# Second stage, first pass: the float32 weights of the products down are asked for after the next pair's first products up

## The chip, the cores and the metric

One core of one Trainium2 chip runs the whole program. The metric is the device time of one execution in microseconds (us), the median of several runs.

## The reference

Linear attention with an exponential feature map, then a two-layer network with a leaky activation, then a mixture of four experts whose outputs are weighted per token. The change lies in the last part:

```python
def _moe2_ref(x, domain_probs, w1, w2):
    N, D = x.shape              # 2304, 512
    E = w1.shape[0]             # 4 experts of 1024 hidden units
    p = domain_probs / (domain_probs.sum(-1, keepdims=True) + 1e-09)
    out = np.zeros((N, D), dtype=np.float32)
    for e in range(E):
        h = np.maximum(x @ w1[e], 0.0)
        out += p[:, e:e + 1] * (h @ w2[e])
    return out
```

## The kernel before

The program has two stages: attention and the first network, then the four experts. The second stage goes over the 2304 tokens in three passes (i = 0, 1, 2) of 768 tokens, each as two halves r of 384. The 4096 hidden units of all experts are 32 chunks of 128. Two chunks form one f (0 to 15), two f form a pair gp (0 to 7), so a pair has a group of four chunks.

`up2(i, f)` (L923) computes the hidden values of two chunks for both token halves with seven products in place of eight, in the order 1, 5, 6, 2, 7, 3, 4. Each is six matmuls of TensorE (L934) into a bank of PSUM. Products 1, 6, 7 and 4 add up in one bank (pb), 5 and 3 in another (pd). In between ScalarE copies partial sums out: p1 (L952) before product 6 may write that bank again, p5 (L955), and u1 (L958) before product 7. VectorE adds them (`total`, L947) to c11, c22 and c12; c22 reads pb before product 4 writes there. `down2(i, gp, r, ...)` (L969) multiplies the hidden values of a pair by its four chunks of weights down (L981) and adds the result, scaled per token, to the output (L990, L992).

All operands are split into a rounded high part and a low rest, so every weight exists twice. In the first pass the weights come as float32: `weights_down(0, c)` (L859) loads a chunk into a raw tile (L867; written `w<-wdn` in the rows), ScalarE casts it to the high part, VectorE subtracts to get the low part (`split`, L237 and L240), and both are stored to DRAM for the later passes (L1020). `weights_up(0, f)` (L824) does the like for an f with two loads into raw tiles (L835), seven casts on ScalarE (L843) and eleven operations on GpSimd (L844 to L854). The raw tiles of both come from one pool of five (L759). The finished weights down of a group go into one of two sets of four places (`down_place`, L811): chunks 8k to 8k+4 into tiles named whd and wld, 8k+5 to 8k+7 into a part of Xh, so the casts into `Xh<-w` are of such chunks. Later passes load the finished weights (L830, L864).

The order of instructions on each engine is set when the program is built, by a scheduler that goes by the order in which the source asks for the work, and takes what is ready in its own reckoning. SP issues all loads and stores in one order. The main loop (L1015 to L1034) asks, for each f: up2, the weights up of f + 2, the stores that are due, then a down2 of one half; after the odd f it asks for the four chunks of the next pair.

Of the kernel before, what the change touches and what calls it, by code (L numbers as in the profile page):

```python
# [41 lines left out]
NPAIR = E * NF2 // 2  # L42
# [161 lines left out]
def fused(ctx: ExitStack, tc: tile.TileContext, qT, kT, v_main, v_tail, w_phi, alpha, probs, w64, wup, wdn, out):  # L204
# [30 lines left out]
    def split(src, hi, lo, hi_eng, lo_eng):  # L235
        if hi_eng is nc.scalar:
            nc.scalar.copy(hi, src)  # L237
        else:
            hi_eng.tensor_copy(hi, src)
        lo_eng.tensor_tensor(lo, src, f32(hi), ALU.subtract)  # L240
# [97 lines left out]
    with ExitStack() as st1:  # L338
# [232 lines left out]
        for p in range(len(pairs)):  # L571
# [44 lines left out]
            for h in range(3):  # L616
                pr_ = RANK["Q"] + p + 0.1 * h
                pm, n = (("pmt", (p,)), 1) if h == 2 else (("pmq", (p, h)), NM)
# [161 lines left out]
    def inputs(i, part):  # L780

        a = lambda r, c: acc_of(slice(2 * c, 2 * c + 2), (2 * i + r) * BLK2, BLK2)
        tt = nc.vector.tensor_tensor
        if part == 0:
            x_op(1, a(0, 0))
            x_op(4, a(1, 1))
            tt(a(1, 1), a(1, 0), a(1, 1), ALU.add)
            x_op(5, a(1, 1))
            tt(a(1, 0), a(1, 0), a(0, 0), ALU.subtract)
            tt(a(0, 0), a(1, 1), a(0, 0), ALU.subtract)  # L790
            x_op(6, a(0, 0))
            x_op(2, a(0, 1))
            tt(a(0, 1), a(0, 1), a(0, 0), ALU.subtract)
        else:
            x_op(7, a(1, 0))
            x_op(3, a(0, 1))
# [14 lines left out]
    def down_place():  # L811

        at = turn[1] % 8
        turn[1] += 1
        if at < 5:
            p_ = wa[1] if at < 4 else wb[1]
            return [p_.tile([P, DM], F32R, name="w" + n + "d") for n in "hl"]
        o = 16 * BLK2 + (at - 5) * 2 * DM
        return [XF[:, o + r * DM:o + (r + 1) * DM] for r in range(2)]

    def raw_tile():
        return rpool.tile([P, DM], F32, name="w")

    def weights_up(i, f):  # L824

        w = {k: up_place().rearrange("p (r c) -> p r c", r=2) for k in SEQ}
        uw[i, f] = w
        if i:
            for j, k in enumerate(SEQ):
                nc.sync.dma_start(f32(w[k]).rearrange("p r c -> p (r c)"), wsu[f][:, j])  # L830
            return
        b = {}
        for r in range(2):
            t = raw_tile()
            nc.sync.dma_start(t, wup[f, :, r])  # L835
            for n, h in zip(((11, 21), (22, 12))[r], range(2)):
                b[n] = t[:, h * 2 * P:(h + 1) * 2 * P]
        sums = [wtpool.tile([P, DM], F32, name=f"ts{r}") for r in range(2)]
        lo = lambda k: sums[k // 6][:, k % 2 * 2 * P:(k % 2 + 1) * 2 * P]
        tt = nc.gpsimd.tensor_tensor  # L840

        def parts(k, src):
            nc.scalar.copy(w[k][:, 0], src)  # L843
            tt(w[k][:, 1], src, f32(w[k])[:, 0], ALU.subtract)  # L844
            stores.append((f, wsu[f][:, SEQ.index(k)], f32(w[k]).rearrange("p r c -> p (r c)")))

        parts(1, b[11])
        tt(lo(5), b[12], b[11], ALU.subtract)
        tt(lo(6), b[22], lo(5), ALU.subtract)
        parts(5, lo(5))  # L850
        tt(lo(4), b[21], lo(6), ALU.subtract)
        parts(6, lo(6))
        parts(2, b[21])
        tt(lo(7), b[12], b[22], ALU.subtract)  # L854
        parts(7, lo(7))
        parts(3, b[22])
        parts(4, lo(4))

    def weights_down(i, c):  # L859
        w = down_place()  # L860
        dw[i, c] = w
        if i:
            for r in range(2):
                nc.sync.dma_start(f32(w[r]), wsd[c][:, r])  # L864
            return
        t = raw_tile()
        nc.sync.dma_start(t, wdn[c])  # L867
        split(t, *w, nc.scalar, nc.vector)
        for r in range(2):
            stores.append((c // 4 * 2 + 1, wsd[c][:, r], f32(w[r])))  # L870
# [13 lines left out]
    for s, (grp, blk) in enumerate(steps):  # L884
# [5 lines left out]
        for i in range(1, GRP):  # L890
# [7 lines left out]
            if todo and (blk or s == 0) and not (grp == 0 and len(todo) <= 2):  # L898
                n, half = todo.pop(0)
# [23 lines left out]
    def up2(i, f):  # L923
        ps = {k: None for k in ("pa", "pb", "pd")}
        t = lambda name: tpool.tile([P, BLK2], F32, name=name)
        w = uw.pop((i, f))

        def product(k, name, start, stop):
            if start:
                ps[name] = ps_u.tile([P, BLK], F32, name="up")[:, :BLK2]  # L930
            n = 0
            for kt in range(2):
                for r, x in ((0, 0), (0, 2), (1, 0)):
                    nc.tensor.matmul(ps[name], w[k][:, r, kt * P:(kt + 1) * P], slots[k][:, x + kt],  # L934
                                     start=start and n == 0, stop=stop and n == 5, skip_group_check=True)
                    n += 1

        def g(c, r, src):
            o = free.pop(0)
            gh, gl = (o[:, j * BLK2:(j + 1) * BLK2] for j in range(2))  # L940
            nc.scalar.activation(gh, src, AF.Relu)  # L941
            nc.vector.scalar_tensor_tensor(gl, src, 0.0, f32(gh), ALU.max, ALU.subtract)  # L942
            gs[2 * f + c, r] = gh, gl, o

        def total(name, x, out):
            o = t(out)
            nc.vector.tensor_tensor(o, ps[name], x, ALU.add)  # L947
            return o

        product(1, "pb", True, False)  # L950
        p1 = t("p1")
        nc.scalar.copy(p1, ps["pb"])  # L952
        product(5, "pd", True, False)
        p5 = t("p5")
        nc.scalar.copy(p5, ps["pd"])  # L955
        product(6, "pb", False, False)
        u1 = t("u1")
        nc.scalar.copy(u1, ps["pb"])  # L958
        product(2, "pa", True, True)
        g(0, 0, total("pa", p1, "c11"))  # L960
        product(7, "pb", False, False)
        c22 = total("pb", p5, "c22")
        product(3, "pd", False, True)
        g(1, 0, total("pd", u1, "c12"))
        product(4, "pb", False, True)
        g(0, 1, ps["pb"])
        g(1, 1, c22)

    def down2(i, gp, r, by_tile):  # L969

        chunks = range(4 * gp, 4 * gp + 4)
        ps = {}

        def product(c, m):
            if c == chunks[0]:
                ps[m] = ps_d.tile([P, BLK], F32, name="dn")
            gh, gl, _ = gs[c, r]
            wh, wl = dw[i, c]
            sl = slice(m * P, (m + 1) * P)
            for k, (w, x) in enumerate(((wh, gh), (wl, gh), (wh, gl))):  # L980
                nc.tensor.matmul(ps[m], x[:, sl], w, start=c == chunks[0] and k == 0, stop=c == chunks[-1] and k == 2)  # L981

        def add2(m):
            tok = (2 * i + r) * TB + m
            if (gp, r, m) == (0, 0, 0):
                acc2[i] = apool.tile([P, 2 * TB, DM], F32, name="acc2")
            av = acc2[i][:, r * TB + m]
            pe = pr[:, tok, 2 * gp // EP:2 * gp // EP + 1]
            if gp == 0:
                nc.vector.tensor_scalar_mul(av, ps[m], pe)  # L990
            else:
                nc.vector.scalar_tensor_tensor(av, ps[m], pe, av, ALU.mult, ALU.add)  # L992
            if gp == NPAIR // 2 - 1:
                nc.sync.dma_start(out[tok * P:(tok + 1) * P], av)

        if by_tile:
            for m in range(TB):
                for c in chunks:
                    product(c, m)
                add2(m)  # L1000
        else:
            for c in chunks:
                for m in range(TB):
                    product(c, m)
            for m in range(TB):
                add2(m)
        for c in chunks:
            free.append(gs.pop((c, r))[2])

    ups = [(i, f) for i in range(NPASS) for f in range(NPAIR)]  # L1010
# [3 lines left out]
    for n, (i, f) in enumerate(ups):  # L1014
        gp = f // 2  # L1015
        up2(i, f)
        if n + 2 < len(ups):
            weights_up(*ups[n + 2])
        while stores and stores[0][0] <= n + 1:
            nc.sync.dma_start(*stores.pop(0)[1:])  # L1020
        if f % 2 == 0:
            if gp:
                down2(i, gp - 1, 1, False)
        else:
            down2(i, gp, 0, False)
            if n + 1 < len(ups):
                i2, f2 = ups[n + 1]
                for c in range(4):
                    weights_down(i2, 2 * f2 + c)
            if gp == NPAIR // 2 - 1:  # L1030
                down2(i, gp, 1, True)
                if i + 1 < NPASS:
                    inputs(i + 1, 0)
                    inputs(i + 1, 1)  # L1034
# [39 lines left out]
```

## Time and profile before

| | us |
|---|---|
| median of 3 runs (1321.79 to 1323.01) | 1322.16 |
| the profiled execution | 1321.2 |
| its span, first to last instruction | 1319.1 |
| TensorE busy with matmuls | 1307.2 (99%) |
| VectorE, ScalarE, GpSimd busy | 758.1, 454.6, 274.2 |
| matmuls of the products up and down, second stage, in the chain that ended last | 25% and 29% of the span |

The second stage's first pass runs from about 566 to 819 us of the span. A matmul's shown duration overlaps the next one's, so the pace is read from the distance between starts. In the rows PE is TensorE, DVE VectorE, ACT ScalarE, POOL GpSimd, and SPq an entry of SP's DMA queue.

### The profile page before, as it was taken

How to read it: one execution, taken by the hardware profiler on the slowest of the kernel's cores; microseconds unless marked ns; L12 is line 12 of the kernel's file. 1: busy time of each engine (PE TensorE's matmuls, PEld its weight loads, DVE VectorE, ACT ScalarE, POOL GpSimd, SP SyncE). 2: the span in 40 equal slices, each digit the busy share in tenths (PEclk: the TensorE clock that was granted, in tenths of full speed). 3: DMA queues.
4: the chain of work that ended last, by engine and by line, in shares of the span. 5: the costliest groups of instructions: out<-in, count | busy, mean ns of one | idle time of the engine just before them, and what ended most of it. 6: DMA issues, size and time to landing. Idle time of an engine off the chain costs nothing.

```text
span 1319.1 us, 21240 instructions
## 1 busy us (share of the span) xinstructions
PE 1307.2 (99%) x8184; PEld 1118.5 (85%) x8184; DVE 758.1 (57%) x1283; ACT 454.6 (34%) x979; POOL 274.2 (21%) x292
## 2 busy tenths in 40 slices
PE   9999999999999999998999999999999999999998
PEld 5577776888888888897999998999999899999997
DVE  7996866999697456664455446433343453333433
ACT  6775655332131121253444433222222232222221
POOL 5562412120020130274566620000000000000000
PEclk9999999999999999999999999999999999999999
DMA  5431220322020030098677666666666565566641
GB/s 168 123 110 49 55 56 12 112 81 96 17 72 9 9 119 1 25 320 287 246 254 257 251 221 197 227 188 194 195 188 192 176 224 175 176 186 190 192 135 48
DMA packets 102469, 192.36 MB, mean 146 GB/s; under 512 B 13920, under 2 KB 14048, under 8 KB 102368
## 3 DMA queue, kind: packets, MB, share of 16 engines
q1 hardware_dynamic: 102368, 191.00, 44.5%
q8 instruction: 65, 1.06, 0.3%
q14 instruction: 36, 0.29, 0.1%
HBM read 140.10 MB, written 50.86 MB: 145 GB/s over the span
## 4 chain that ended last, share of the span: by engine, by line
PE 93%; DVE 3%; DMA 1%; ACT 1%; issue 1%; SPq 0%; POOL 0%; DVEq 0%; ACTq 0%; POOLq 0%
PE dn L981 29%; PE up L934 25%; PE up L292 12%; PE dn L313 12%; PE mm L313 3%; PE mm L292 2%; PE kv L447 2%; PE bank L522 2%; PE bank L403 2%; DVE m L419 1%; PE bank L532 1%; PE bank L503 1%; DMA w<-wdn 1%; PE kv L456 0%; DVE pmk L425 0%
## 5 line engine op out<-in xcount | busy, mean ns | idle before, releaser
L981 PE MATMUL dn<-whd,Xh 128*128 128x512 f32 x720 | 231.4, 390 | 0.0
L992 DVE SCALAR_TENSOR_TENSOR acc<-dn,pr,acc 128x512 f32<-128x512 f32 x126 | 88.7, 749 | 190.9 <-PE dn L981 190.9
L934 PE MATMUL up<-Xl,wlu 128*128 128x384 f32 x864 | 158.8, 335 | 2.7 <-DVE c L947 2.6
L981 PEld LDWEIGHTS dn<-whd,Xh 128*128 128x128 f32 x720 | 135.1, 188 | 27.1
L934 PEld LDWEIGHTS up<-Xl,wlu 128*128 128x128 f32 x864 | 150.2, 188 | 4.3 <-DVE c L947 3.8
L947 DVE TENSOR_TENSOR c<-up,p 128x384 f32<-128x384 f32 x96 | 53.5, 557 | 174.1 <-PE up L934 171.5
L981 PE MATMUL dn<-Xh 128*128 128x512 f32 x648 | 151.8, 389 | 0.0
L981 PEld LDWEIGHTS dn<-Xh 128*128 128x128 f32 x648 | 121.6, 188 | 25.5
L981 PE MATMUL dn<-wld,Xh 128*128 128x512 f32 x360 | 140.8, 391 | 0.0
L952 ACT COPY p<-up 128x384 f32<-128x384 f32 x48 | 23.1, 481 | 325.7 <-PE up L934 325.6
L934 PE MATMUL up<-Xl,whu 128*128 128x384 f32 x576 | 111.7, 334 | 1.1 <-ACT p L952 1.1
L941 ACT ACTIVATE Xh<-c 128x384 fp32r<-128x384 f32 x144 | 75.6, 526 | 80.0 <-DVE c L947 80.0
L934 PEld LDWEIGHTS up<-Xl,whu 128*128 128x128 f32 x576 | 101.2, 188 | 1.4 <-ACT p L952 1.4
L292 PE MATMUL up<-Xl,whu 128*128 128x512 f32 (+1 forms) x272 | 99.1, 364 | 0.0
L292 PE MATMUL up<-Xh,whu 128*128 128x512 f32 (+1 forms) x272 | 99.1, 364 | 0.0
L313 PE MATMUL dn<-gh,wld 128*128 128x512 f32 (+1 forms) x272 | 99.1, 364 | 0.0
L313 PE MATMUL dn<-gh,whd 128*128 128x512 f32 (+1 forms) x272 | 99.1, 364 | 0.0
L313 PE MATMUL dn<-gl,whd 128*128 128x512 f32 (+1 forms) x272 | 99.0, 364 | 0.0
L292 PE MATMUL up<-Xh,wlu 128*128 128x512 f32 (+1 forms) x272 | 99.0, 364 | 0.0
L942 DVE SCALAR_TENSOR_TENSOR Xh<-c,Xh 128x384 fp32r<-128x384 f32 x144 | 86.0, 599 | 5.4
L237 ACT CAST gh<-t 128x512 fp32r<-128x512 f32 (+1 forms) x68 | 38.6, 569 | 145.1 <-DVE t L304 143.0
L981 PEld LDWEIGHTS dn<-wld,Xh 128*128 128x128 f32 x360 | 67.5, 188 | 13.0
(171 smaller groups left out, 2222.4 us busy)
## 6 DMA issues: line engine op xcount, KB each, us to landing
whu<-wsu SPq DMA_DIRECT2D x96, 256.0 KB, 3.4
wlu<-wsu SPq DMA_DIRECT2D x96, 256.0 KB, 3.1
st<-w SPq DMA_DIRECT2D x24, 512.0 KB, 3.2
wsu<-whu SPq DMA_DIRECT2D x48, 256.0 KB, 3.1
wsu<-wlu SPq DMA_DIRECT2D x48, 256.0 KB, 2.3
Xh<-wsd SPq DMA_DIRECT2D x48, 256.0 KB, 3.8
wld<-wsd SPq DMA_DIRECT2D x40, 256.0 KB, 3.0
whd<-wsd SPq DMA_DIRECT2D x40, 256.0 KB, 3.3
```

The lines of the kernel that those rows point to most:

```text
L237: nc.scalar.copy(hi, src)
L292: nc.tensor.matmul(ps[:, :bn], a[:, cs], x[:, cc, t0:t0 + bn], start=n == 0, stop=n == 3 * CC - 1)
L313: nc.tensor.matmul(ps, w[:, sl], g, start=start and k == 0, stop=stop and k == 2)
L403: nc.tensor.matmul(ps[h][:, i], x[r, i * P:(i + 1) * P], w0[r, h], start=True, stop=True, tile_position=(h * D, 0), skip_group_check=True)
L447: nc.tensor.matmul(kv[h * D + o:h * D + o + 32, 0], a[:, o:o + 32], e, start=i == 0, stop=i == NM, tile_position=(0, h * D + o), skip_grou ...
L522: nc.tensor.matmul(nd[o:o + 32, :HS], tl["kvt", p][:, a:a + 32], tl["qe", p][:, h, s, c * HS:(c + 1) * HS], start=s == 0, stop=s == 1, til ...
L934: nc.tensor.matmul(ps[name], w[k][:, r, kt * P:(kt + 1) * P], slots[k][:, x + kt], start=start and n == 0, stop=stop and n == 5, skip_grou ...
L941: nc.scalar.activation(gh, src, AF.Relu)
L942: nc.vector.scalar_tensor_tensor(gl, src, 0.0, f32(gh), ALU.max, ALU.subtract)
L947: nc.vector.tensor_tensor(o, ps[name], x, ALU.add)
L981: nc.tensor.matmul(ps[m], x[:, sl], w, start=c == chunks[0] and k == 0, stop=c == chunks[-1] and k == 2)
L992: nc.vector.scalar_tensor_tensor(av, ps[m], pe, av, ALU.mult, ALU.add)
```

## The change

In the first pass, the four chunks of pair gp are asked for after up2 of its even f, after the weights up of f + 2 and the stores, ahead of the second down2 of pair gp - 1. Before, they were asked for after the first down2 of pair gp - 1, so ahead of that up2. The first pass's pair 0 and the later passes are asked for as before.

```diff
         if f % 2 == 0:
+            if gp and i == 0:
+                for c in range(4):
+                    weights_down(i, 4 * gp + c)
             if gp:
                 down2(i, gp - 1, 1, False)
         else:
             down2(i, gp, 0, False)
-            if n + 1 < len(ups):
+            if n + 1 < len(ups) and (i or gp == NPAIR // 2 - 1):
                 i2, f2 = ups[n + 1]
                 for c in range(4):
                     weights_down(i2, 2 * f2 + c)
```

On TensorE the order stays as it was. Three places show what moves, all for chunks 12 to 15, whose conversion falls around up2 of f = 5.

SP's queue, before, from the load of chunk 12 to that of chunk 15. `w<-wdn` is the load of a chunk, `wsu6<-` and `wsd12<-` are stores of finished weights; in brackets stand the counters that the entry waits for (DMAHW: an earlier transfer; Pool, Activation, DVE: work of GpSimd, ScalarE, VectorE).

```order
L867 DMA w_7190<-wdn 128x512 [waits DMAHW2_49]
L1020 DMA wsu6_63<-whu_6955 128x512 [waits DMAHW3_49,Pool_49]
L1020 DMA wsu6_63<-whu_6956 128x512 [waits DMAHW4_49,Pool_49]
L1020 DMA wsu6_63<-wlu_6957 128x512 [waits DMAHW5_49,Pool_49]
L1020 DMA wsu6_63<-wlu_6958 128x512 [waits DMAHW6_49,Pool_49]
L867 DMA w_7194<-wdn 128x512 [waits DMAHW7_49]
L1020 DMA wsu6_63<-wx_6959 128x512 [waits DMAHW0_49,Pool_49]
L1020 DMA wsu6_63<-wx_6960 128x512 [waits DMAHW1_49,Pool_49]
L867 DMA w_7198<-wdn 128x512 [waits DMAHW2_49]
L1020 DMA wsu6_63<-whu_6961 128x512 [waits DMAHW3_49,Pool_49]
L1020 DMA wsd12_85<-whd_7188 128x512 [waits DMAHW4_49,Activation_49]
L867 DMA w_7202<-wdn 128x512 [waits DMAHW5_49,DVE_49]
```

The same place after, from the second store of wx to behind the load of chunk 14.

```order
L1020 DMA wsu6_63<-wx_6936 128x512 [waits DMAHW1_49,Pool_49]
L867 DMA w_7293<-wdn 128x512 [waits DMAHW2_49]
L1020 DMA wsu6_63<-whu_6937 128x512 [waits DMAHW3_49,Pool_49]
L1020 DMA wsd12_85<-whd_7291 128x512 [waits DMAHW4_49,Activation_49]
L867 DMA w_7297<-wdn 128x512 [waits DMAHW5_49,DMAHW2_49,DVE_49]
L1020 DMA wsd12_85<-wld_7292 128x512 [waits DMAHW6_49]
L1020 DMA wsd13_86<-Xh_122 128x512 [waits DMAHW7_49,Activation_49]
L867 DMA w_7301<-wdn 128x512 [waits DMAHW5_49,DMAHW0_49,DVE_49]
L1020 DMA wsu7_64<-whu_7100 128x512 [waits DMAHW1_49,Pool_49]
```

The first load moved behind the stores of wx, and the second and third now wait for VectorE: each goes into the raw tile that the chunk before it has left. The fourth load (not shown) stands behind six stores of f = 7.

ScalarE, before, at the start of up2 of f = 5: casts of chunks 12 to 15, then that up2's copies.

```order
L237 CAST whd_7188<-w_7190 128x512
L237 CAST Xh_122<-w_7194 128x512
L237 CAST Xh_122<-w_7198 128x512
L237 CAST Xh_122<-w_7202 128x512
L952 COPY p1_7050<-up_7043 128x384
L843 CAST whu_7108<-w_7115 128x256
L955 COPY p5_7059<-up_7052 128x384
L843 CAST whu_7109<-ts0_7119 128x256
L958 COPY u1_7067<-up_7043 128x384
```

The same place after.

```order
L237 CAST whd_7291<-w_7293 128x512
L237 CAST Xh_122<-w_7297 128x512
L952 COPY p1_7042<-up_7035 128x384
L843 CAST whu_7100<-w_7107 128x256
L955 COPY p5_7051<-up_7044 128x384
L843 CAST whu_7101<-ts0_7111 128x256
L958 COPY u1_7059<-up_7035 128x384
L843 CAST whu_7102<-ts1_7112 128x256
L237 CAST Xh_122<-w_7301 128x512
```

The cast of chunk 14 moved behind the copies, that of chunk 15 further back; chunks 12 and 13 are still ahead of p1.

VectorE, before, there: subtractions of chunks 12 to 15, three evictions of a down2 (L992), and the sums of up2.

```order
L240 TENSOR_TENSOR wld_7189<-w_7190,whd_7188 128x512
L240 TENSOR_TENSOR Xh_122<-w_7194,Xh_122 128x512
L240 TENSOR_TENSOR Xh_122<-w_7198,Xh_122 128x512
L992 SCALAR_TENSOR_TENSOR acc2_6546<-dn_7001,pr_119,acc2_6546 128x512
L992 SCALAR_TENSOR_TENSOR acc2_6546<-dn_7005,pr_119,acc2_6546 128x512
L992 SCALAR_TENSOR_TENSOR acc2_6546<-dn_7009,pr_119,acc2_6546 128x512
L240 TENSOR_TENSOR Xh_122<-w_7202,Xh_122 128x512
L947 TENSOR_TENSOR c11_7076<-up_7069,p1_7050 128x384
L947 TENSOR_TENSOR c22_7086<-up_7043,p5_7059 128x384
```

The same place after.

```order
L240 TENSOR_TENSOR wld_7292<-w_7293,whd_7291 128x512
L992 SCALAR_TENSOR_TENSOR acc2_6546<-dn_6993,pr_119,acc2_6546 128x512
L992 SCALAR_TENSOR_TENSOR acc2_6546<-dn_6997,pr_119,acc2_6546 128x512
L992 SCALAR_TENSOR_TENSOR acc2_6546<-dn_7001,pr_119,acc2_6546 128x512
L240 TENSOR_TENSOR Xh_122<-w_7297,Xh_122 128x512
L947 TENSOR_TENSOR c11_7068<-up_7061,p1_7042 128x384
L240 TENSOR_TENSOR Xh_122<-w_7301,Xh_122 128x512
L947 TENSOR_TENSOR c22_7078<-up_7035,p5_7051 128x384
```

The subtraction of chunk 13 moved behind the evictions, that of chunk 14 between c11 and c22. Chunks 16 to 19, 20 to 23 and 24 to 27 read the same at f = 7, 9 and 11; chunks 28 to 31 keep the old order. For chunks 4 to 7 (up2 of f = 2) three casts stand ahead of p1 and the fourth ahead of p5; for chunks 8 to 11 (f = 3) one cast stands ahead of p1.

## Rows read from the trace of the kernel before

**Rows 1.** The page, part 1: busy us, share of the span, instructions.
```profile
PE 1307.2 (99%) x8184; PEld 1118.5 (85%) x8184; DVE 758.1 (57%) x1283; ACT 454.6 (34%) x979; POOL 274.2 (21%) x292
```
**Rows 2.** Windows: length; busy PE, PEld, DVE, ACT, POOL (count); clock; DMA share; GB/s.
```profile
604.40:616.00 11.60, 7.90 (x43) 7.22 (x43) 5.81 (x11) 6.60 (x16) 4.12 (x5) 1.00 0.65 230
616.00:800.00 184.00, 184.00 (x925) 166.66 (x925) 87.01 (x138) 76.13 (x176) 92.92 (x112) 1.00 0.71 249
```
**Rows 3.** Timeline of PE, f = 3: start, duration, operation, [idle before, releaser].
```profile
604.44 1.23 PE L934 MATMUL up<-x,whu 128*128 128x384 f32 x6
...
607.82 1.31 PE L934 MATMUL up<-Xl,whu 128*128 128x384 f32 x6 [1.10 <-ACT p L952]
...
614.85 1.31 PE L934 MATMUL up<-Xl,wlu 128*128 128x384 f32 x6 [2.60 <-DVE c L947]
```
**Rows 4.** Timeline of ACT, f = 3.
```profile
605.58 1.81 ACT L237 CAST whd<-w 128x512 fp32r<-128x512 f32 x3 [8.35 <-DMA w<-wdn]
607.29 0.47 ACT L952 COPY p<-up 128x384 f32<-128x384 f32 x1
...
612.99 0.62 ACT L237 CAST whd<-w 128x512 fp32r<-128x512 f32 x1 [2.98 <-DMA w<-wdn]
```
**Rows 5.** Timeline of DVE, f = 3.
```profile
613.64 0.69 DVE L240 TENSOR_TENSOR wld<-w,whd 128x512 fp32r<-128x512 f32 x1 [2.80 <-ACT whd L237]
```
**Rows 6.** The chain of waits around f = 3: start, duration, what.
```profile
600.58 4.92 DMA w<-wdn
...
607.83 5.13 DMA w<-wdn
```
**Rows 7.** Timeline of PE, f = 2: products 1; 6 and 2; 7 and 3.
```profile
588.94 1.23 PE L934 MATMUL up<-x,whu 128*128 128x384 f32 x6
...
591.04 2.24 PE L934 MATMUL up<-Xl,wlu 128*128 128x384 f32 x12
593.12 2.24 PE L934 MATMUL up<-Xl,wx 128*128 128x384 f32 x12
```
**Rows 8.** Timeline of ACT, f = 2.
```profile
591.67 0.41 ACT L843 CAST whu<-ts 128x256 fp32r<-128x256 f32 x1
592.34 0.48 ACT L958 COPY u<-up 128x384 f32<-128x384 f32 x1 [0.26 <-PE up L934]
```
**Rows 9.** Timeline of PE, f = 5, product 1.
```profile
639.71 1.23 PE L934 MATMUL up<-x,whu 128*128 128x384 f32 x6
```
**Rows 10.** Timeline of SP's queue ahead of f = 5.
```profile
631.34 2.35 SPq L1020 DMA_DIRECT2D wsu<-wx  x2
633.74 0.42 SPq L867 DMA_DIRECT2D w<-wdn  x1
```
**Rows 11.** Timeline of ACT, f = 5.
```profile
641.03 0.48 ACT L952 COPY p<-up 128x384 f32<-128x384 f32 x1 [0.49 <-PE up L934]
```
**Rows 12.** Timeline of DVE, f = 5: three evictions, and c22.
```profile
639.14 2.06 DVE L992 SCALAR_TENSOR_TENSOR acc<-dn,pr,acc 128x512 f32<-128x512 f32 x3
...
645.19 0.56 DVE L947 TENSOR_TENSOR c<-up,p 128x384 f32<-128x384 f32 x1 [0.47 <-PE up L934]
```
**Rows 13.** Line 867, one load, issued at 664.8: issue ns; us to landing.
```profile
L867 SPq DMA_DIRECT2D w<-wdn x1: 426/426/426, 664.8 to 664.8; - x1
...
DMA to landing us min/median/max: 3.2/3.2/3.2
```
**Rows 14.** Line 867, four loads in a row, chunks 4 to 7.
```profile
L867 SPq DMA_DIRECT2D w<-wdn x4: 328/426/451, 576.2 to 581.9; - x4
...
DMA to landing us min/median/max: 2.7/3.0/3.4
```
**Rows 15.** Timeline of POOL: an L854, and the end of f = 3's part.
```profile
573.06 0.74 POOL L854 TENSOR_TENSOR ts<-w 128x256 f32<-128x256 f32 x1 [0.66 <-DMA w<-wup]
...
583.82 1.18 POOL L844 TENSOR_TENSOR wlu<-ts,wlu 128x256 fp32r<-128x256 f32 x1
```
**Rows 16.** Timeline of SP's queue: the last store of f = 4.
```profile
600.21 0.32 SPq L1020 DMA_DIRECT2D wsu<-whu  x1
```

## The prediction, made before the run

> **What bounds the kernel now.** I read the page's busy times first: TensorE (PE) is busy 1307.2 us of the span [rows 1], so only idle time of PE can be taken away, and any new idle time of PE is paid in full. Next the windows of the second stage's first pass: from 616 to 800 us PE is busy 184.00 of 184.00 us, and from 604.4 to 616 us it is busy 7.90 of 11.60, with the granted clock at 1.00 in both [rows 2]. So 3.70 us is all that the first pass has to give. The timeline of PE names the two holes, both inside the products up of pair-half f = 3: 1.10 us until ScalarE's copy p, and 2.60 us until VectorE's c [rows 3]. The timeline of ScalarE shows why: three casts of float32 weights of products down stand ahead of the copy p and start only when their load has landed, and a fourth holds ScalarE again at 612.99 [rows 4]; its subtraction on VectorE ends just before the late c [rows 5]. The chain of waits gives the loads: 4.92 us and 5.13 us [rows 6]. The reader should keep this picture, since the change makes more of it: **a cast ahead of p, or a subtraction ahead of c, hands a late load to PE.**
>
> How much slack there is: a call of up2 is seven products of 6 matmuls, one every 1.04 us. In f = 2 they begin at 588.94, the third at 591.04 and the fifth at 593.12 [rows 7]. The third reuses the bank of copy p, the fifth that of copy u, the seventh that of c22. The copy u starts 3.40 us into that call and takes 0.48 us, with the fifth product 4.18 us in [rows 7, 8]. So PE waits as soon as p, u or c22 comes some 0.2 to 0.3 us later than now.
>
> **The change, part by part.** PE's order and its work don't change, nor do sizes or counts of loads, casts, subtractions and stores. Only the requests of chunks 4 to 27 move behind later work, and the listings show three consequences.
>
> *Raw tiles.* There are five, shared with the weights up. Now weights up for two further halves are requested first and hold four of them. So the load of the second chunk of a group of four waits for VectorE's subtraction of the first chunk, and the third for that of the second: load, cast, subtract, load, cast, subtract, load, one after the other. Before, loads two and three of chunks 12 to 14 waited for no engine's work.
>
> *The copy p.* In the groups of chunks 12, 16, 20 and 24 two casts stand ahead of p (four before), but the second now belongs to a load that starts late.
>
> *The sum c22.* VectorE has the third chunk's subtraction between c11 and c22; before, all four stood ahead of c11.
>
> The chunks 28 to 31 keep the old order.
>
> **One group of four, worked out** (chunks 12 to 15, in the products up of f = 5, which begin at 639.71 [rows 9]). By the spacing above the third product is due at 639.71 + 2.10 = 641.81, the seventh at 639.71 + 6.26 = 645.97. The first load now follows the second store of wx. In the trace those stores are issued from 631.34 on, and the next entry, a load, stands at 633.74 [rows 10]. A cast takes 0.62 us [rows 4], the copy p 0.48 [rows 11], a subtraction 0.69 [rows 5], c22 0.56, and the three evictions ahead of the second subtraction end at 641.20 [rows 12]. For a load from issue to landing I take 3.2 us: that is the load in just this slot at 664.8, behind one store [rows 13]. Bounds: 2.7 us, the shortest of four loads in a row [rows 14], and 4.9 to 5.1 us [rows 6]. I take the near one because the loads of a group are now apart instead of in threes. Then: landing 636.94, cast 637.56, subtraction 638.25, second load lands 641.45, cast 642.07, p 642.55: PE waits 0.74. Second subtraction 642.76, third load lands 645.96, cast 646.58, subtraction 647.27, c22 647.83, due 645.97 + 0.74 = 646.71: PE waits 1.12. Together **1.9 us**, four times **7.5 us**. With 2.7 us per load the copy p is in time, the second subtraction starts at 641.20 behind the evictions, and c22 is some 0.6 us late, so 2.6 us for four. Every further us per load adds two to the first wait and one to the second: at 4.9 us a group costs 1.9 + 3 x 1.7 = 7.0.
>
> **The first group** (chunks 4 to 7, products up of f = 2). Before, its loads began at 576.2 [rows 14], ahead of the stores of f = 3's weights up; now they follow the seventh of them. GpSimd ends that part at 583.82 + 1.18 = 585.00 [rows 15]; one more operation of 0.74 us [rows 15] is now ahead of it, so 585.74, and with the store's own issue the loads begin at 586.1, 586.5 and 587.0. Landing from 589.3, three casts in 1.81 us [rows 4], p at 591.6, due at 591.04: 0.5 us. The fourth load waits for the first subtraction (589.92 + 0.69 = 590.61) and lands at 593.81; its cast (594.43) now stands ahead of the copies p5 and u; with those two at 0.48 and a cast of 0.41 between [rows 8], u ends at 595.8, due at 593.12 + 0.5: 2.1 us. Together **2.7 us** (1.7 at 2.7 us per load, 6.1 at 4.9, since two loads stand in the chain to u).
>
> **The second group** (chunks 8 to 11), where the holes are now: one cast stands ahead of p, and no subtraction between c11 and c22, so **3.7 us** go. Its first load follows the last store of f = 4, which came at 600.21, 7.4 us after the copy u ended at 592.82 [rows 8, 16]. With u at 595.8 that is 603.2, two loads more before it put it near 604.7, landing 607.9, cast 608.5; p may start at 604.44 + 2.7 + 1.6 = 608.7. So it fits, with 1.5 us of wait as the other bound at 4.9 us per load.
>
> **What lies elsewhere costs nothing:** the stores of the halves are issued one step later on SP, but the second pass reads them hundreds of us later; the products down of a group need its weights some 30 us after the casts. The cover for these is PE's own work from 616 to 800 us [rows 2]; if it were gone, the first products down of a pair would wait, which nothing here comes near.
>
> **Sum.** -3.7 + 2.7 + 7.5 = +6.5 us. The profiled execution took 1321.2 us (span 1319.1), 1.0 below the median of the three runs, 1322.16. I put the sum on the median: 1328.7 us.
>
> **Rivals.** *Faster: the holes go and nothing follows.* If a load took 2.2 us, c22 would be only 0.1 us late in each of the four groups and the first group would cost about 0.7 us, which makes -3.7 + 0.7 + 0.4 = -2.6, or 1319.6 us; the sign turns near 2.6 us. For it: the loads now come one by one, with fewer transfers beside them. Against: none of the loads shown is under 2.7 us [rows 13, 14].
>
> *No change: short loads.* At 2.7 us the sum is -3.7 + 1.7 + 2.6 = +0.6, or 1322.8 us. For it: 2.7 occurs in this trace [rows 14]. Against: the slot that matters shows 3.2 [rows 13]. The Trainium skill, page "DMA: Bandwidth & Descriptors", section "Anatomy of one DMA — SWDGE (gpsimd) path", gives a fixed 2.0 us and the bytes over 436 GB/s, for loads issued by GpSimd; for 256 KB that is 2.6 us, an estimate by that page, and by it the time would be about 1322.5 us. The loads here are issued by SP, and the trace shows longer ones.
>
> *Much slower: loads as slow as the ones that made the holes.* At 3.6 us the groups cost 3.1 each the first group 3.5, and the sum is near +12, or 1334 us; at 4.9 us it is near +32, or 1354. For it: exactly this order of casts cost 3.70 us with such loads [rows 3, 6]. Against: those stood behind two loads of weights up and among stores.
>
> **How the numbers follow.** Loads near 3.2 us (1325 to 1332 us): 0.60. Much slower (over 1332): 0.20. No change: 0.12. Faster: 0.08. About 0.2% (2.6 us) is what a measurement of this kernel can tell from no change. So slower 0.80, same 0.12, faster 0.08. The range from 1322 to 1337 us leaves out the faster case and the far end of the slow one.
>
> **What would show it.** In the profile after: windows with idle PE spread over the first pass; waits of the products up for ScalarE's p and VectorE's c in f = 5, 7, 9 and 11, near 1 us each, and for u in f = 2; no wait in f = 3; loads of one group some 4.5 us apart, each right behind a subtraction. I am wrong if PE stays full from 616 to 800 us, if f = 13, whose order is unchanged, waits too, if the second or third load is issued before the subtraction, or if the granted clock falls behind a wait.

## The result and the profile after

The changed kernel took **1329.32 us** (median of 6 runs, 1328.52 to 1333.04), the kernel before in the same comparison 1322.35 us (6 runs, 1321.79 to 1323.01). The ratio is 1.0062 with a 95% interval from 1.0051 to 1.0072: slower by 7.0 us by the medians, where 6.5 us were forecast. The profiled execution took 1328.52 us, with a span of 1326.7 us, 7.6 us more than the span of before.

The page's busy times, part 1 of the profile after, answer to [rows 1]:

```profile
PE 1309.0 (99%) x8184; PEld 1117.8 (84%) x8184; DVE 756.8 (57%) x1283; ACT 452.9 (34%) x979; POOL 272.9 (21%) x292
```

The work is the same: TensorE (PE) executes as many instructions in the same time, within 1.8 us. What grew is its idle time. The windows show where; first three stretches of before, cut anew (length; busy PE, PEld, DVE, ACT, POOL with counts; granted clock; DMA share; GB/s):

```profile
560.00:604.00 44.00, 43.87 (x247) 40.74 (x246) 26.31 (x42) 22.13 (x54) 33.35 (x41) 1.00 0.93 324
604.00:620.00 16.00, 12.30 (x63) 10.88 (x62) 8.00 (x14) 7.63 (x18) 7.95 (x10) 1.00 0.64 229
620.00:800.00 180.00, 180.00 (x908) 163.36 (x907) 85.22 (x135) 75.10 (x173) 89.09 (x108) 1.00 0.72 250
```

and the same stretches after:

```profile
560.00:604.00 44.00, 42.59 (x240) 39.49 (x239) 24.70 (x41) 22.32 (x54) 33.00 (x41) 1.00 0.85 303
604.00:620.00 16.00, 13.91 (x71) 12.46 (x70) 8.04 (x13) 7.18 (x17) 8.02 (x10) 1.00 0.72 235
620.00:800.00 180.00, 174.78 (x868) 156.01 (x867) 81.86 (x132) 71.07 (x168) 88.39 (x108) 1.00 0.71 244
```

Idle PE of 0.13, 3.70 and 0.00 us became 1.41, 2.09 and 5.22. The first stretch lost, the second gained, and the third, full before, has the new holes. Timeline of PE after (start, duration, operation, [idle before, releaser]), in f = 2, f = 3 and f = 5:

```profile
594.84 2.38 PE L934 MATMUL up<-Xl,wx 128*128 128x384 f32 x12 [1.04 <-ACT u L958]
...
610.66 1.31 PE L934 MATMUL up<-Xl,whu 128*128 128x384 f32 x6 [2.09 <-ACT p L952]
...
639.68 1.23 PE L934 MATMUL up<-x,whu 128*128 128x384 f32 x6
...
642.38 1.31 PE L934 MATMUL up<-Xl,whu 128*128 128x384 f32 x6 [0.43 <-ACT p L952]
...
647.47 1.33 PE L934 MATMUL up<-Xl,wlu 128*128 128x384 f32 x6 [0.65 <-DVE c L947]
648.64 0.40 PE L981 MATMUL dn<-whd,Xh 128*128 128x512 f32 x1
```

The two waits of f = 5, for p and for c, come again in f = 7, 9 and 11. Two rows of f = 11 show the largest wait for c:

```profile
740.35 1.32 PE L934 MATMUL up<-Xl,whu 128*128 128x384 f32 x6 [0.23 <-ACT p L952]
...
746.39 1.33 PE L934 MATMUL up<-Xl,wlu 128*128 128x384 f32 x6 [1.60 <-DVE c L947]
```

A word on counting. Ends of matmuls are modelled, so the idle time written beside a row is less than what the stretch grew by. In f = 5 the products up of before ran from 639.71 [rows 9] to the first product down at 647.02, 7.31 us; after, from 639.68 to 648.64, 8.96 us: 1.65 us more, beside 1.08 us of idle rows. So I count by the shift of the first product down behind each group's products up, before against after. It stands at +0.5 us ahead of f = 2 (580.74 before, 581.25 after), +1.9 behind f = 2 (596.24, 598.10), 0.0 behind f = 3 (616.00, 615.97), then +1.6, +3.5, +5.1 and +7.5 behind f = 5, 7, 9 and 11 (740.06, 747.56), and stays at 7.5. **The first two groups give nothing in sum; the four groups cost 7.5 us.**

Why p and c are late there is in two other views. Timeline of ACT after, f = 5, and timeline of DVE after:

```profile
636.98 0.62 ACT L237 CAST whd<-w 128x512 fp32r<-128x512 f32 x1 [4.52 <-DMA w<-wdn]
641.33 0.62 ACT L237 CAST Xh<-w 128x512 fp32r<-128x512 f32 x1 [3.72 <-DMA w<-wdn]
641.86 0.47 ACT L952 COPY p<-up 128x384 f32<-128x384 f32 x1
645.60 0.62 ACT L237 CAST Xh<-w 128x512 fp32r<-128x512 f32 x1 [1.03 <-DMA w<-wdn]
```

```profile
646.26 0.69 DVE L240 TENSOR_TENSOR Xh<-w,Xh 128x512 fp32r<-128x512 f32 x1 [0.86 <-ACT Xh L237]
646.86 0.55 DVE L947 TENSOR_TENSOR c<-up,p 128x384 f32<-128x384 f32 x1
```

The second cast has waited 3.72 us for its load, with p right behind it; the third subtraction has waited for the third cast, with c22 right behind it. The chain of waits after names the loads, and SP's queue after shows the store ahead of the second:

```profile
633.71 3.20 DMA w<-wdn
...
637.64 0.70 DVE wld L240
...
638.36 2.90 DMA w<-wdn
```

```profile
637.63 0.32 SPq L1020 DMA_DIRECT2D wsd<-whd  x1
638.36 0.33 SPq L867 DMA_DIRECT2D w<-wdn  x1
```

The third is issued at 642.70. The loads are 4.65 and 4.34 us apart, each issued as the subtraction of the chunk before it ends: load, cast, subtraction, load. SP's queue has a part in this chain too: the entry ahead of the second load is the store of the first chunk's high part, which waits for the cast and goes out at 637.63. The load waits for VectorE itself only from then on, some 0.4 us. So the late place in SP's queue, behind that store, holds the load too.

### The profile page after: what moved, and what is told of

Read it like the earlier page. It is cut to its first block, busy times and chain, and to the rows that moved or that the text cites. A ratio compares the mean times of both kernels' runs of the same rounds, so it can differ in the third digit from the quotient of the medians.

```text
span 1326.7 us, 21237 instructions
## 1 busy us (share of the span) xinstructions
PE 1309.0 (99%) x8184; PEld 1117.8 (84%) x8184; DVE 756.8 (57%) x1283; ACT 452.9 (34%) x979; POOL 272.9 (21%) x292
## 3 DMA queue, kind: packets, MB, share of 16 engines
q8 instruction: 65, 1.06, 0.3%
## 4 chain that ended last, share of the span: by engine, by line
PE 88%; DVE 3%; DMA 3%; issue 2%; ACT 1%; POOL 1%; SPq 1%; POOLq 0%; ACTq 0%; DVEq 0%
PE dn L981 27%; PE up L934 23%; PE up L292 12%; PE dn L313 12%; PE mm L313 3%; PE mm L292 2%; PE kv L447 2%; PE bank L522 2%; DMA w<-wdn 2%; PE bank L403 2%; PE bank L532 1%; DVE m L419 1%; PE bank L503 1%; DMA wsu<-whu 1%; PE kv L456 0%
## 5 line engine op out<-in xcount | busy, mean ns | idle before, releaser
L992 DVE SCALAR_TENSOR_TENSOR acc<-dn,pr,acc 128x512 f32<-128x512 f32 x126 | 88.9, 750 | 167.1 <-PE dn L981 167.1
```

## The experiments

My theory: the loss is this chain. With the weights up of two halves requested first, too few raw tiles are left for a group, so its loads wait for VectorE, and the fixed order of casts and subtractions hands them to PE. Rivals: the move of the first two groups costs; the place of the loads on SP's queue, behind stores, costs; being requested behind the products up costs by itself. Every run is timed against the kernel before in the same comparison: median 1321.30 us for the first four, 1321.16 for the last three. Stage figures are shifts as above.

**Only the four groups (and chunks 28 to 31).** Against the changed kernel:

```diff
-            if gp and i == 0:
+            if i == 0 and gp in (3, 4, 5, 6, 7):
...
-            if n + 1 < len(ups) and (i or gp == NPAIR // 2 - 1):
+            if n + 1 < len(ups) and (i or gp + 1 not in (3, 4, 5, 6, 7)):
```

> Only the groups of chunks 12, 16, 20 and 24 (and 28) are requested late; chunks 4 to 11 keep the order of before. Theory (the loss is the chain of load, cast, subtraction, next load in the four groups): the holes of f = 3 stay as before (1.1 and 2.6 us), the four groups cost the 7.5 us that the changed kernel shows from f = 5 to f = 11, so 7 to 8 us over the kernel before, about 1329.9 us: slightly slower than the whole change. Rival one (the cost is in the move of the first two groups, what follows only drifts): within 1.5 us of the kernel before. Rival two (later loads collide with others wherever they are): between 2 and 5 us over it.

Measured: 1328.48 us, ratio 1.0049 (1.0035 to 1.0062), 7.2 us over before by the medians. The shift grows by 7.7 us from behind f = 3 to behind f = 11, nothing in f = 2. Some 0.7 of the 7.7 us is no wait: the clock fell behind f = 3's old hole (see the last section), between 614 and 618 us. So the four groups alone cost about as much as the whole change.

**Only the first two groups.** The same two lines with `(1, 2)` in place of `(3, 4, 5, 6, 7)`.

> Only chunks 4 to 11 are requested late; from chunk 12 on the order is that of before. Theory: the three shifts that the changed kernel shows there (+0.5 in f = 1, +1.3 in f = 2, -1.9 in f = 3) sum to -0.1, so within 1 us of the kernel before, and TensorE without an idle row from f = 4 on. Rival one: 6 to 8 us slower than before. Rival two: 1 to 4 us slower.

Measured: 1321.69 us, ratio 1.0004 (0.9995 to 1.0013): no difference. Windows of this run:

```profile
616.00:800.00 184.00, 184.00 (x925) 166.66 (x925) 90.41 (x142) 77.87 (x179) 94.86 (x113) 1.00 0.73 254
```

PE is full from 616 us on, as in [rows 2]. The shift is 0.0 ahead of f = 2, f = 2 adds 1.1 us and f = 3 another 0.1, where the changed kernel won 1.9. Timeline of PE in f = 3 and windows of 2 us over it:

```profile
610.33 2.08 PE L934 MATMUL up<-Xl,whu 128*128 128x384 f32 x6 [2.46 <-ACT p L952]
```

```profile
610.00:612.00 2.00, 1.67 (x6) 1.67 (x7) 0.63 (x1) 1.27 (x4) 1.34 (x2) 0.65 0.53 166
612.00:614.00 2.00, 2.00 (x8) 2.00 (x7) 0.00 (x0) 0.78 (x2) 0.72 (x2) 0.50 0.92 341
```

The six matmuls behind the wait took 2.08 us instead of 1.31, while the granted clock fell to 0.50. The rival of the first groups falls. The first term of the shifts falls too: the order in f = 1 is the changed kernel's, and the +0.5 us ahead of f = 2 is not there, so it wasn't the change's; in the seven runs' profiles it lies between -0.8 and +0.4.

**Seven raw tiles.** The changed kernel with

```diff
-    rpool = pool("raw", 5)
+    rpool = pool("raw", 7)
```

> All requests as in the changed kernel, but seven raw tiles instead of five, so that the first three loads of a group wait for no engine; the loads still stand behind the stores of the weights up. Theory: the cost of the four groups goes, no wait of TensorE for p or c from f = 5 to f = 11; f = 3 has its three casts ahead of p and one subtraction between c11 and c22 again, so its holes of 3.7 us come back, less or more by up to 1.5; f = 2 costs up to 1.3: in sum 0 to 3 us over the kernel before, about 1323.5 us. Rival three (it is the later place of the loads on SP, behind the stores, that costs, not the raw tiles): the waits in f = 5 to 11 stay near 1.9 us a group and the time stays within 1.5 us of the changed kernel's 1329.3.

Measured: 1321.61 us, ratio 0.9999 (0.9990 to 1.0008). All waits of PE for the products up from 561 to 830 us (total us, times, longest us):

```profile
PE up L934 <- ACT p L952: 4.0, 2, 2.2
```

Both are in f = 2 and f = 3, none in the four groups; their shift is 0.0 us instead of 7.5. So the cost hangs on the number of raw tiles. But the loads do not stand as late on SP as I expected. SP's queue ahead of f = 5, the loads of chunks 12 and 13:

```profile
625.70 0.46 SPq L867 DMA_DIRECT2D w<-wdn  x1
...
632.23 0.45 SPq L867 DMA_DIRECT2D w<-wdn  x1
```

Less the shift of 1.9 us, that is where they stood before (623.18 and 630.30), and not behind the stores of wx (633.71). With tiles to spare the scheduler gave the loads their old places back. So the rival of the place on SP is not settled by this run: the late place and the wait for a raw tile went together, and no run has one without the other. Both come from too few raw tiles. What f = 2 lost was more than I said: all four casts stand ahead of p there, and it cost 2.1 us instead of up to 1.3.

**Six raw tiles.** The same line with `6`. This one tells a chain ahead of p from a mere count of tiles.

> All requests as in the changed kernel, six raw tiles instead of five: in the four groups the first two loads wait for no engine, the third waits for the first subtraction and the fourth for the second, and all four casts stand ahead of the copy p, none behind it. Theory (what counts is the chain that stands ahead of p and of c22, not how many tiles there are): the third and fourth load land near 641.3 and 641.9 us of the old time axis with loads of 2.9 to 3.2 us, their casts end near 642.5, p 1.1 to 1.4 us late, c22 in time: 4.4 to 5.6 us for the four groups, with some 1 to 2 us net in f = 2 and f = 3 about 6 us over the kernel before, waits of TensorE in f = 5 to 11 for p alone and none for c. Rival (the cost falls with each tile more): half of the changed kernel's 7.5 us, 3 to 4 us over before, with waits for p and for c. Rival (only three loads in a chain cost): as with seven tiles, within 1.5 us of before.

Measured: 1326.69 us, ratio 1.0037 (1.0024 to 1.0049), so about 5.5 us lost: most of the loss is still there with one tile more. The four groups shift by 1.40, 1.42, 1.16 and 0.99 us, 5.0 in sum (4.4 to 5.6 expected). Waits of PE for the products up, 561 to 830 us, and the chain of waits in f = 5 (start, duration, what):

```profile
PE up L934 <- ACT p L952: 7.5, 6, 2.6
PE up L934 <- DVE c L947: 1.2, 1, 1.2
```

```profile
638.33 0.70 DVE Xh L240
...
639.05 3.62 DMA w<-wdn
...
642.75 0.04 ACT Xh L237
...
643.27 0.48 ACT p L952
```

The six waits for p are one in each of f = 2, 3, 5, 7, 9 and 11; the one wait for c is in f = 3. As the theory has it, c22 is in time in the four groups and p pays for four casts: the chain goes from a subtraction to the last load, its cast and p. Neither rival has p alone waiting.

**Requested behind the products up, but ahead of the weights up.** Against the kernel before (the old requests are left out for these groups):

```diff
         up2(i, f)
+        if i == 0 and f % 2 == 0 and gp in (1, 2, 3, 4, 5, 6, 7):
+            for c in range(4):
+                weights_down(i, 4 * gp + c)
         if n + 2 < len(ups):
             weights_up(*ups[n + 2])
```

> The requests stand behind the products up of the even pair-half, as in the changed kernel, but ahead of the weights up of the next halves, so that these take the raw tiles after them and not before. Theory (only the order in which raw tiles are handed out counts): casts and subtractions stand where they stood before, no load of a group but the fourth waits for an engine, within 1 us of the kernel before, the two holes of f = 3 included. Rival (being requested behind the products up costs by itself): 2 to 7 us slower than before.

Measured: 1322.20 us, ratio 1.0003 (0.9994 to 1.0012): no difference, and no wait of PE from f = 5 on. The edit moves the same requests behind the same products up; what it doesn't move is the weights up. So being behind the products up is free, and what costs is being behind the weights up, which then hold the raw tiles.

**Only chunks 8 to 11.** The two lines of the first run with `(2,)`.

> Only the group of chunks 8 to 11 is requested late. Theory: f = 3 has one cast ahead of p and gains 1.9 to 3.7 us, nothing else moves: 1 to 4 us faster than the kernel before, about 1319.5 us, and so faster than both. Against it: the subtraction of chunk 9 stands between c11 and c22 in f = 3, behind a load that waits for the subtraction of chunk 8; if that comes late as in f = 5 (about 1 us), the gain shrinks to 1 to 2 us. Rival one (late requests of the first groups cost): 1 us slower than before or more.

Measured: 1319.23 us, ratio 0.9983 (0.9974 to 0.9991): faster than both kernels, than the one before by 2.1 us at the medians, in the lower half of the 1 to 4 us that I gave. Timeline of PE, f = 3, and of SP's queue (start, issue time):

```profile
607.82 1.32 PE L934 MATMUL up<-Xl,whu 128*128 128x384 f32 x6 [0.87 <-ACT p L952]
...
613.02 1.34 PE L934 MATMUL up<-Xl,wlu 128*128 128x384 f32 x6 [0.75 <-DVE c L947]
```

```profile
601.34 0.92 SPq L835 DMA_DIRECT2D w<-wup  x2
602.30 0.43 SPq L867 DMA_DIRECT2D w<-wdn  x1
```

Both waits are left in small. The load of chunk 8 stands behind two loads of weights up, and the second of the group waits for the first subtraction.

**Chunk 8 as before, chunks 9 to 11 late.** Against the kernel before:

```diff
+            if i == 0 and f == 4:
+                for c in (9, 10, 11):
+                    weights_down(i, c)
             if gp:
                 down2(i, gp - 1, 1, False)
...
                 for c in range(4):
-                    weights_down(i2, 2 * f2 + c)
+                    if i2 or 2 * f2 + c not in (9, 10, 11):
+                        weights_down(i2, 2 * f2 + c)
```

> The kernel before, with one edit: of chunks 8 to 11 the first is requested as before, the other three behind the products up of f = 4. In f = 3 only the cast of chunk 8 stands ahead of p, and no subtraction between c11 and c22; all else as before. Theory: chunk 8's load starts behind the loads of f = 4's or f = 5's weights up as in the fourth run, so p may still be 0 to 1 us late, and c22 is in time: 3 to 4 us faster than before, about 1318 us, and 0.5 to 1.5 us faster than with the whole group late, TensorE with one idle row at most in f = 3. If the load of chunk 8 takes 4.5 us or more from a start at 602 us, a wait of 1 us or more for p remains and the time is that of the fourth run.

Measured: **1316.71 us**, ratio 0.9963 (0.9951 to 0.9976), 4.5 us below the kernel before by the medians and the fastest here. That is more than the 3 to 4 us expected, and the lead over the whole group late, some 2.4 us when each is set against before, is more than the 0.5 to 1.5. Its windows, SP's queue and ACT:

```profile
560.00:604.00 44.00, 44.00 (x248) 41.01 (x247) 26.36 (x42) 22.18 (x54) 33.32 (x41) 1.00 0.91 325
604.00:620.00 16.00, 16.00 (x82) 14.51 (x81) 9.30 (x15) 7.78 (x18) 9.43 (x11) 1.00 0.80 272
620.00:800.00 180.00, 180.00 (x910) 163.52 (x909) 88.22 (x141) 77.78 (x177) 87.89 (x106) 1.00 0.72 251
```

```profile
600.72 0.42 SPq L867 DMA_DIRECT2D w<-wdn  x1
601.19 0.97 SPq L835 DMA_DIRECT2D w<-wup  x2
```

```profile
605.06 0.62 ACT L237 CAST whd<-w 128x512 fp32r<-128x512 f32 x1 [8.12 <-DMA w<-wdn]
605.59 0.47 ACT L952 COPY p<-up 128x384 f32<-128x384 f32 x1
```

Now the load of chunk 8 stands ahead of the weights up. It still takes 4.3 us, but it starts at 600.72, so its cast ends at 605.68, and the third product, due at 604.15 + 2.10 = 606.25, isn't kept waiting. PE has no idle time from 560 to 800 us. The holes of f = 3 are gone by moving three requests instead of 24. By the distance of starts they were more than 3.70 us: f = 3 took 11.56 us before (604.44 to 616.00), f = 2, without a wait, 7.30 (588.94 to 596.24), so 4.26 us were there to gain.

## Why the prediction was right

The forecast, 1328.7 us and slower, holds, and so do the place and, in the main, the mechanism of the loss. That the sum came so near is in part luck. Point by point:

- **The four groups: 7.5 us forecast, 7.5 us measured** (1.65, 1.85, 1.62 and 2.41). The working of f = 5 holds step by step. First cast ended at 637.56 forecast, 637.60 measured; second 642.07 and 641.95; copy p 642.55 and 642.33; third subtraction 647.27 and 646.95; c22 647.83 and 647.41. The loads took 3.20 and 2.90 us where I took 3.2. In f = 11 the third load took 3.8 us (issued at 740.67), c22 came later, and PE waits 1.60 us for it there. So the sum agrees better than its parts: three groups a little under 1.9, one over. The working has each load wait for VectorE's subtraction alone. The store on SP ahead of it, which waits for the cast, is missing there; it holds the load until some 0.4 us before that subtraction ends.
- **The first group: +2.7 forecast, +1.3 measured.** The mis-sized step is "with the store's own issue the loads begin at 586.1 ... Landing from 589.3". They began at 585.80, and the first landed after 2.78 us instead of 3.2, so p was in time, where I had 0.5 us. The fourth load then went out at 589.97, not 590.61, and u ended at 594.79 instead of 595.8. The wait for u is where it was forecast, half as long. Some 0.5 us of the difference is none of these steps: f = 2 itself began at 589.46 instead of 588.94, so p and u were due that much later.
- **The second group: -3.7 forecast, -1.9 measured.** The mis-sized step is "landing 607.9": the load was issued at 605.09 (604.7 forecast) and took 4.45 us, not 3.2. PE waited 2.09 us for p. The bound of 1.5 us at 4.9 us per load was stated and was nearer. My working took the price of a load from a later place in the first pass, although [rows 6] show slow loads in this very place. That those stood behind two loads of weights up was misread: on SP the load at 600.58 stands behind stores, with two more of its group behind it, and the loads of weights up nearest to the one at 607.83 come after it, at 608.33. The term of 3.7 us was itself too small by 0.56, since the idle rows understate the holes (4.26 us by the distance of starts).
- **These two errors, -1.4 and +1.8, partly cancel.** With the 0.5 us ahead of f = 2 they leave +0.9 in this profile, beside a four-group sum that was right. That they cancel is luck. The second run, which has these two groups alone, shows their sum, between -0.7 and +1.7 us by its interval, some of it the clock's, where I had -1.0.
- No wait in f = 13, no load issued before its subtraction, clock 1.00 in the profiled execution: the points that would have made the prediction wrong didn't come. "No wait in f = 3" was wrong.
- One sum of a rival is a little off: at 2.7 us per load the rows give c22 at 641.20 + 0.69 + 2.7 + 0.62 + 0.69 + 0.56 = 646.46, due 645.97, so 0.5 us late and not 0.6. That makes 2.0 us for four groups, and the rival's sum near 0 instead of +0.6. The forecast doesn't use it.

Two rows for the second and third point, SP's queue after, and the chain of waits after:

```profile
603.54 1.50 SPq L835 DMA_DIRECT2D w<-wup  x2
605.09 0.48 SPq L867 DMA_DIRECT2D w<-wdn  x1
```

```profile
585.80 2.78 DMA w<-wdn
...
605.09 4.45 DMA w<-wdn
```

The rival of short loads fell on its price: over all loads of line 867 in the profile after the median is 3.1 us, from 2.5 to 5.2. The Trainium skill, page "DMA: Bandwidth & Descriptors", section "Anatomy of one DMA — SWDGE (gpsimd) path", gives a formula for loads issued by GpSimd, by which 256 KB take 2.6 us, an estimate. The loads here are issued by SP; the trace has 2.6 us near its lower end, and its median of 3.1 doesn't agree.

## What to carry to other kernels

Where a pool of landing tiles is shared, the order of requests can decide whose loads run beside each other and whose run one after another: count the tiles held by what is requested first, then follow load, last reader, next load as one chain up to the engine that has no slack, with the entries that stand between them in the queue. Move as few requests as the hole needs: here three requests of one group gained 4.5 us, while moving 24 lost 7. And take a load's price from a row in the same place of the program. The first load of the group for f = 3 took 4.9 us before (600.58), 4.45 behind two loads of weights up in the changed kernel, and 4.3 ahead of them in the last run, where the first loads of the four groups in the changed kernel took 3.0 to 3.2. So the entry just ahead of it in the queue is not what makes it slow; what does stays open.

## What the runs showed that I had not expected

The granted clock of TensorE fell behind waits of some 2 us. In the profile of the first run, PE waited 1.06 and then 1.89 us in f = 3, and the last six matmuls of the stretch took 2.17 us instead of 1.31 [rows 3]. Timeline and windows of that run:

```profile
614.44 2.17 PE L934 MATMUL up<-Xl,wlu 128*128 128x384 f32 x6 [1.89 <-DVE c L947]
```

```profile
612.00:614.00 2.00, 0.55 (x4) 0.23 (x2) 0.77 (x2) 1.42 (x4) 0.42 (x1) 1.00 1.03 397
614.00:616.00 2.00, 1.56 (x5) 1.56 (x6) 1.95 (x5) 1.56 (x4) 1.92 (x3) 0.65 0.41 158
616.00:618.00 2.00, 2.00 (x6) 1.71 (x6) 1.50 (x2) 0.78 (x2) 2.00 (x3) 0.50 0.39 150
```

It is the lower level, 1.2 GHz instead of 2.4, for some 3 us, and cost about 1.5 us: f = 3's waits were 0.75 us shorter than in [rows 3], and yet the shift grew by 0.8 us from 604.77 (604.44 before) to 625.34 (624.20 before). The same happened in the profiles of the second run, of the one with seven raw tiles and of the one requested ahead of the weights up, behind waits of 2.0 to 2.5 us. It did not happen in the profile of before, behind 2.60 us, nor in that after, behind 2.09 us, nor in that with six raw tiles, behind 2.63 us. So the length of a wait alone doesn't tell, and the price of a wait of some 2 us in this stretch differs by some 1.5 us between these profiles. What decides stays open; no run here tried it. Part of the gain of the last version may be that no wait is left for the clock to fall behind: among executions with a mean granted clock of 1.000 it is 3.9 us faster than the kernel before (median 1316.61 of 3 against 1320.53 of 7), where all together give 4.5.
